# Value weights in two loads from ScalarE's queue, gate columns behind the first of them, first values in row steps

## The chip, the cores and the metric

One core of a Trainium2 chip runs the kernel. The metric is the device time of one execution in microseconds (us); the time before is 221.36, the median of three runs (221.32 to 221.83). The profile is of one execution, which took 221.32. Its times count from the first instruction; TensorE is PE, VectorE DVE, ScalarE ACT, GpSimd POOL and SyncE SP.

## What is computed

A block with two branches on one normalised input, in bf16: linear attention with a softmax feature map, and a gated bilinear unit.

```python
# x 2048 x 512, 32 heads of 16; wqkv 512 x 1536; w_gate, w_up 512 x 1792; w_down 1792 x 512
xn = layernorm(x)
q, k, v = split(xn @ wqkv)                          # 32 heads each
phi(a) = concat(softmax(a @ w_phi), softmax(-(a @ w_phi)))
kv = phi(k).T @ v ;  z = sum of phi(k) over tokens
A = (phi(q) @ kv / (phi(q) @ z + 1e-6)) @ wo
B = ((xn @ w_gate) * (xn @ w_up)) @ w_down
out = x + A + B
```

## The kernel before

**Tiles and stages.** The 2048 tokens are 16 tiles `t` of 128; the model dimension of 512 is four row blocks `q` of 128. `x_tile(t)` is loaded, normalised into `xn_tile(t)` and transposed into `xnT`, which every projection reads as its stationary or its moving operand. The values of a tile are `k_pe(t)` (L547): four matmuls of 512 columns over the four row blocks of `wv_v`, the value columns of `wqkv`, and a copy on ACT. The features of the keys need `Wp`, the key weights times `w_phi`: `wprime(1)` (L491) makes it from the transposed key weights `wT` and the block matrix `wbd` (from `w_phi`, `make_wbd`, L391). Then `k_pk(t)` and `k_norm(t)` make softmax features, `emit_kv` sums them with the values, and `q_pk` to `q_oT` do the queries. `glu(g, ft)` (L575) makes 128 of the 1792 hidden columns for 512 tokens: four matmuls with gate columns, four with up columns, a copy of the gate product on ACT, a multiply on DVE (L588). `final(t)` does both output products. There are 56 such gated units, put between the other work to fill TensorE.

**The first four tiles.** Tiles 0 to 3 (`RAW = 4`) are treated apart, to start early: `emit_centred(t)` (L416) subtracts the mean only, `emit_T(t)` (L472) transposes on TensorE with the identity `ident` and copies on ACT, and 1/sqrt(variance) is a scale of the later copies. The mean comes from DVE's statistics, `emit_moments` (L412: `bn_stats` L413 and `bn_aggr` L414), but for the tiles of `ACT_MEAN` (L410: 1 and 3) from an accumulating ACT pass (L421), and `emit_moments` follows later. Tiles 4 to 15 are normalised fully (statistics L450, L479) and transposed by DMA on SP's queue (L483).

**Zero matmuls.** 27 matmuls of zeros (L367) run on TensorE before the first data, and 8 more after the transpose of tile 1 (L724).

**The loads.** L352 to L362 issue all early loads on SP's queue. `load_x(on, t0, n, at)` loads n tiles of x, `load_w` a weight, `load_gu(on, f0, n, at)` n blocks of 128 gate columns and as many up columns (two loads), `load_wT` the key or query weights through a transposing DMA. `at` is the time in ns at which a load is said to land; it is used by the planner alone.

**The order of the work.** Nothing is ordered by hand. Every operation is a step with an engine, a cost, and dependencies from what it reads and writes; steps can be given more of them (`deps.append`). `_order` (L790) then plays the steps through: each engine is free at 850 ns at first, and takes from its steps whose dependencies are already placed the one that can start first, `max(ready, free)`, and of equal ones the one of lowest priority number (mostly the order of writing; gated units have numbers above a million and so come last). A DMA holds its queue for its `issue` cost (500 ns, 4600 ns for `load_wT`) and lands at the later of start plus 1700 ns and `at`. Steps marked `urgent`, the first four tiles' centring and transposes, are taken if they can start within 300 ns of the best one (`URGENT`, L792). The result is a fixed program for each engine, run in order with waits on semaphores (`_emit_all`): an engine whose next instruction waits does nothing else.

Of the kernel before, what the change touches and what calls it, by code (L numbers as in the profile page):

```python
# [12 lines left out]
PE, ACT, DVE, POOL, SP = "PE", "ACT", "DVE", "POOL", "SP"  # L13
# [7 lines left out]
NQ = D // 128  # L21
# [176 lines left out]
def _build(nc, es, A_x, A_wqkv, A_w_phi, A_wo, B_w_gate, B_w_up, B_w_down, out):  # L198
# [59 lines left out]
    def sbv(name, lo, n):  # L258
        off = layout[name] + lo
        return arena[:, off:off + n]  # L260
# [5 lines left out]
    def bank(b, lo=0, n=512):  # L266
        return psum[:, b * 512 + lo: b * 512 + lo + n]

    sc = _Sched(nc)


    def act_op(out_ap, in_ap, func=ACTF.Copy, scale=1.0, bias=None, prio=None):
        def fn(e):
            kw = {}
            if bias is not None:
                kw["bias"] = bias
            return e.activation(out=out_ap, in_=in_ap, func=func, scale=scale, **kw)  # L277
        r = [in_ap]
        if isinstance(scale, bass.AP):
            r.append(scale)  # L280
        if isinstance(bias, bass.AP):
            r.append(bias)
        return sc.step(ACT, fn, reads=r, writes=[out_ap], cost=(50.0 if str(in_ap.tensor.name) == "ps" else 95.0) + 0.833 * in_ap.free_size(),
                       lat=180.0, prio=prio)

    def dve(fn, reads, writes, n, rate=1.0, fixed=65.0, prio=None):
        return sc.step(DVE, fn, reads=reads, writes=writes, cost=fixed + rate * n / 0.96, lat=150.0, prio=prio)

    def pool(fn, reads, writes, n, rate=1.8, fixed=130.0, prio=None):
        return sc.step(POOL, fn, reads=reads, writes=writes, cost=fixed + rate * n, lat=120.0, prio=prio)  # L290

    def mms(items, prio=None, cold=False):

        def fn(e):
            ins = None
            for o, l, r, a, z in items:
                ins = e.matmul(o, lhsT=l, rhs=r, start=a, stop=z)  # L297
            return ins
        reads = []
        writes = []  # L300
        c = 0.0
        for o, l, r, a, z in items:
            reads += [l, r]
            writes.append(o)
            c += max(25.0, o.free_size() / 2.4 + 2.3) * (1.92 if cold else 1.0)
        return sc.step(PE, fn, reads=reads, writes=writes, cost=c, lat=260.0, prio=prio)

    def group(o, pairs):
        n = len(pairs)
        return [(o, l, r, i == 0, i == n - 1) for i, (l, r) in enumerate(pairs)]  # L310

    ident = sbv("ident", 0, 128)
    bind8 = sbv("bind8", 0, 8)
# [5 lines left out]
    def x_tile(t):  # L319
        return sbv("x", t * 512, 512)  # L320
# [3 lines left out]
    def xnT(q, s_lo, n):  # L324
        return sbv("xnT", q * S_TOK + s_lo, n)

    wT_v = sbv("wT", 0, 2 * NQ * 512).rearrange("p (w j d) -> p w j d", w=2, j=NQ)
    wv_v = sbv("wv", 0, NQ * 512).rearrange("p (q j) -> p q j", q=NQ)
# [7 lines left out]
    def load_x(on, t0, n, at):  # L336
        return sc.dma(on, sbv("x", t0 * 512, n * 512).rearrange("p (t d) -> p t d", t=n),
                      x_flat[t0 * 128:(t0 + n) * 128, :].rearrange("(t p) d -> p t d", p=128), at=at)

    def load_w(on, dst, src, at, issue=500.0):  # L340
        return sc.dma(on, dst, src, at=at, issue=issue)
# [5 lines left out]
    def load_gu(on, f0, n, at):  # L347
        return [load_w(on, v[:, :, f0 * 128:(f0 + n) * 128],
                       src[:, f0 * 128:(f0 + n) * 128].rearrange("(q p) f -> p q f", p=128), at)
                for v, src in ((wg_v, B_w_gate), (wu_v, B_w_up))]  # L350

    load_x(SP, 0, 1, 2950.0)  # L352
    load_x(SP, 1, 1, 3400.0)
    load_x(SP, 2, 2, 4700.0)
    load_w(SP, wv_v, A_wqkv[:, 1024:1536].rearrange("(q p) j -> p q j", p=128), 6500.0)
    load_gu(SP, 0, 4, 9900.0)
    load_x(SP, 4, 4, 11400.0)
    sc.dma(SP, wphi_v, bass.AP(tensor=A_w_phi.tensor, offset=A_w_phi.offset, ap=[[16, 128], [2048, NQ], [1, 16]]),
           at=11600.0)
# [5 lines left out]
    zero = sbv("tree", 0, 128)  # L365
# [4 lines left out]
    def c_fn(e):  # L370
        e.memset(ident, 0.0)
        return e.memset(bind8, 1.0)
    pool(c_fn, [], [ident, bind8], 300)

    def c2_fn(e):
        e.affine_select(out=ident, in_=ident, compare_op=ALU.not_equal, fill=1.0, base=0,
# [30 lines left out]

    RAW = 4

    ACT_MEAN = (1, 3)  # L410

    def emit_moments(t):  # L412
        dve(lambda e: e.bn_stats(stats_v[:, t, 0:6], x_tile(t)), [x_tile(t)], [stats_v[:, t, 0:6]], 512)  # L413
# [2 lines left out]
    def emit_centred(t):  # L416

        reads = [x_tile(t)]
        if t in ACT_MEAN:
            mean = lnt_v[:, 2, 8 + t:9 + t]  # L420
# [23 lines left out]
    def scale_of(t):  # L444
        return rstd_v[:, t, 0:1] if t < RAW else 1.0
# [15 lines left out]
    def xn_tile(t):  # L461
        return sbv("xn", (t % 4) * 512, 512)
# [4 lines left out]
    def next_a():  # L467
        b = a_bank[0] % a_banks[0]
        a_bank[0] += 1
        return b  # L470

    def emit_T(t):  # L472
        b = (5, 6, 7, 4)[t] if t < RAW else next_a()
        mms([(bank(b, q * 128, 128), xn_tile(t)[:, q * 128:(q + 1) * 128], ident, True, True) for q in range(NQ)],
            cold=t < 2)
        act_op(xnT_v[:, :, t * 128:(t + 1) * 128], bank(b).rearrange("p (q s) -> p q s", q=NQ))

    def emit_xn(t):
        dve(lambda e: e.tensor_scalar(out=xn_tile(t), in0=x_tile(t), scalar1=mv_v[:, t, 0:1],  # L479
                                      scalar2=rstd_v[:, t, 0:1], op0=ALU.subtract, op1=ALU.mult),  # L480
            [x_tile(t), mv_v[:, t, 0:1], rstd_v[:, t, 0:1]], [xn_tile(t)], 512, rate=0.5)
        if t >= 4:
            sc.dma(SP, xnT_v[:, :, t * 128:(t + 1) * 128], xn_tile(t), transpose=True, issue=1250.0, land=3200.0,  # L483
                   at=36000.0 + 1300.0 * (t - 8) if t >= 8 else 22900.0 + 550.0 * (t - 4))
            return
        emit_T(t)

# [58 lines left out]

    def k_pe(t):  # L547
        b = next_a()
        mms(group(bank(b), [(xnT(q, t * 128, 128), wv_v[:, q, :]) for q in range(NQ)]))
        act_op(vext_all[:, t, :, 0:64], bank(b).rearrange("p (c j) -> p c j", c=8), scale=scale_of(t))  # L550

    def k_pk(t):
# [164 lines left out]
    for t in range(RAW):  # L717
        first = len(sc.steps)
        emit_centred(t)
        emit_T(t)  # L720
        for st in sc.steps[first:]:
            st.urgent = True
        if t == 1:
            mms([(bank(7, 0, 128), zero, zero, True, True)] * 8, cold=True).deps.append(sc.by_eng[PE][-2])  # L724
        if t in ACT_MEAN:
            emit_moments(t)
        emit_root(t)
        k_pe(t)
# [60 lines left out]

def _order(sc):  # L790

    URGENT = 300.0  # L792
    n = len(sc.steps)
    remaining = [len(st.deps) for st in sc.steps]
    dependents = [[] for _ in range(n)]
    for st in sc.steps:
        for d in st.deps:
            dependents[d.idx].append(st)
    ready = {e: [] for e in sc.by_eng}
    ready_time = [0.0] * n  # L800
    for st in sc.steps:
        if remaining[st.idx] == 0:
            ready[st.eng].append((0.0, st.idx))
    free_at = {e: 850.0 for e in sc.by_eng}
    new_order = {e: [] for e in sc.by_eng}
    global_order = []
    for _ in range(n):
        best = None
        for e, lst in ready.items():
            if lst:  # L810
                fa = free_at[e]
                cand = min(lst, key=lambda p: (max(p[0], fa), sc.steps[p[1]].prio))
                soon = [p for p in lst if sc.steps[p[1]].urgent and max(p[0], fa) <= max(cand[0], fa) + URGENT]
                if soon:
                    cand = min(soon, key=lambda p: sc.steps[p[1]].prio)
                key = (max(cand[0], fa), cand[1])
                if best is None or key < best[0]:
                    best = (key, e, cand)
        if best is None:
            raise RuntimeError("scheduling deadlock")  # L820
        (start, idx), e, cand = best
        ready[e].remove(cand)
        st = sc.steps[idx]
        if isinstance(st.lane, tuple):
            free_at[e] = start + st.cost
            st.finish = max(start + st.lat, st.at)
        else:
            free_at[e] = start + st.cost
            st.finish = free_at[e] + st.lat
        st.seq = len(new_order[e])  # L830
        new_order[e].append(st)
        global_order.append(st)
        for dep in dependents[idx]:
            remaining[dep.idx] -= 1
            fin = free_at[PE] if st.lane == PE and dep.lane == PE else st.finish
            ready_time[dep.idx] = max(ready_time[dep.idx], fin)
            if remaining[dep.idx] == 0:
                ready[dep.eng].append((ready_time[dep.idx], dep.idx))
    sc.by_eng = new_order
    sc.est = {e: free_at[e] for e in free_at}  # L840
    return global_order
# [86 lines left out]
```

## Time and profile before

| | us |
|---|---|
| median of three runs | 221.36 |
| the profiled execution | 221.32 |
| its span, first to last instruction | 219.6 |
| TensorE busy | 215.9 (98% of the span), 1285 matmuls |
| VectorE busy | 192.9 (88%), 549 instructions |
| ScalarE busy | 116.7 (53%), 193 instructions |
| GpSimd busy | 10.5 (5%) |
| granted TensorE clock, mean | 1.00 |

Busy time alone says little here, since TensorE is nearly always busy: what tells is when its unbroken row of matmuls begins, when it ends, and what each matmul in it costs. A matmul of 512 columns starts 0.216 us after the one before it when the row is full. One of 128 columns starts 0.107 us after the one before it until 6.7 us, and 0.056 us after it from then on. In the early part the order of instructions on SP's queue, and the time at which each load lands, are read beside it. In the view of DMA issues the last column is the time from issue to landing; in the timeline the first two columns are start and length.

### The profile page before, as it was taken

What the parts mean: (1) busy time and instruction counts of PE and PEld (TensorE: products, weight loads), DVE (VectorE), ACT (ScalarE), POOL (GpSimd) and SP (SyncE); (2) the same over time, 40 slices, a digit from 0 to 9 for tenths busy, and PEclk for the clock granted to TensorE, in tenths of its full rate; (3) what the DMA queues carried; (4) which work ended last, traced back from release to release, by engine and by line L of the source; (5) the groups of instructions that cost most, each with busy time, mean ns of one, the idle gap of its engine ahead of it and who ended that gap; (6) DMA issues with size and microseconds to landing.
All of it is one profiled execution on the core that took longest, in us unless ns stands there. A gap on an engine that the chain in (4) does not pass through costs nothing.

```text
span 219.6 us, 3584 instructions
## 1 busy us (share of the span) xinstructions
PE 215.9 (98%) x1285; PEld 106.1 (48%) x1285; DVE 192.9 (88%) x549; ACT 116.7 (53%) x193; POOL 10.5 (5%) x29
## 2 busy tenths in 40 slices
PE   7999999999999999999999999999999999999995
PEld 7554444444445545444445544444444445444543
DVE  3578999999997489999999899999999999998432
ACT  4868986465533599965452785745453333230000
POOL 4440000200002000000000000000000000000000
DMA  6999630048400440000000003155366555856451
GB/s 165 337 292 285 132 135 0 3 96 280 150 0 4 96 96 3 0 0 0 3 0 1 3 0 59 37 96 102 84 131 99 119 119 118 102 120 142 96 75 49
DMA packets 47442, 19.91 MB, mean 91 GB/s; under 512 B 37440, under 2 KB 47424, under 8 KB 47424
## 3 DMA queue, kind: packets, MB, share of 16 engines
q1 hardware_dynamic: 47424, 19.69, 39.4%
q8 instruction: 10, 0.16, 0.3%
q14 instruction: 8, 0.07, 0.1%
HBM read 8.67 MB, written 2.10 MB: 49 GB/s over the span
## 4 chain that ended last, share of the span: by engine, by line
PE 96%; DMA 2%; DVE 1%; SPq 0%; issue 0%
PE ps L297 96%; DMA arena<-in_A_x_dram 2%; SPq L165 0%; DVE arena L413 0%; DVE arena L428 0%; DVE arena L693 0%; DVE arena L414 0%
## 5 line engine op out<-in xcount | busy, mean ns | idle before, releaser
L297 PE MATMUL ps<-arena 128*128 128x512 bf16 (+4 forms) x1285 | 215.9, 332 | 1.4 <-DVE arena L366 1.0
L297 PEld LDWEIGHTS ps<-arena 128*128 128x128 bf16 x1285 | 106.1, 99 | 111.0 <-ACT arena L277 1.1
L277 ACT ACTIVATE arena<-ps 128x512 bf16<-128x512 f32 (+1 forms) x136 | 72.1, 590 | 46.8 <-PE ps L297 38.7
L277 ACT ACTIVATE arena<-arena 128x1024 bf16<-128x1024 bf16 (+1 forms) x40 | 38.6, 978 | 28.8 <-DVE arena L523 28.7
L537 DVE TENSOR_TENSOR arena<-arena 128x512 f32<-128x512 bf16 (+3 forms) x128 | 48.9, 391 | 0.1
L588 DVE TENSOR_TENSOR arena<-ps,arena 128x512 bf16<-128x512 f32 x56 | 37.9, 677 | 4.4 <-PE ps L297 2.1
L517 DVE TENSOR_TENSOR arena<-arena 128x64 bf16<-128x64 bf16 (+3 forms) x128 | 31.3, 270 | 3.2 <-ACT arena L277 2.9
L523 DVE TENSOR_TENSOR arena<-arena 128x1024 bf16<-128x1024 bf16 x32 | 21.5, 671 | 0.1
L693 DVE TENSOR_TENSOR arena<-ps,arena 128x512 bf16<-128x512 f32 (+2 forms) x13 | 8.4, 647 | 7.1 <-PE ps L297 6.9
L564 DVE TENSOR_TENSOR arena<-arena 128x1024 bf16<-128x1024 bf16 x16 | 10.8, 677 | 0.0
L450 DVE BATCH_NORM_STATS2 arena<-arena 128x6 f32<-128x512 bf16 x12 | 8.0, 678 | 2.3 <-DMA arena<-in_A_x_dram 2.3
L277 ACT ACTIVATE arena<-ps,arena 128x512 bf16<-128x512 f32 x12 | 7.9, 682 | 2.1 <-PE ps L297 1.6
L561 DVE RECIPROCAL arena<-arena 128x64 bf16<-128x64 f32 x16 | 8.7, 541 | 0.0
L665 DVE TENSOR_TENSOR arena<-ps,arena 128x512 bf16<-128x512 f32 x12 | 8.1, 674 | 0.1
L657 DVE RECIPROCAL arena<-ps 128x32 f32<-128x32 f32 x16 | 5.5, 347 | 2.4 <-PE ps L297 2.4
L644 DVE TENSOR_TENSOR arena<-arena 128x512 bf16<-128x512 bf16 x16 | 6.6, 413 | 0.0
L641 DVE RECIPROCAL arena<-arena 128x32 f32<-128x32 f32 x16 | 5.3, 334 | 0.0
L479 DVE TENSOR_SCALAR arena<-arena 128x512 bf16<-128x512 bf16 x12 | 4.2, 405 | 1.1 <-POOL arena L458 1.1
L413 DVE BATCH_NORM_STATS2 arena<-arena 128x6 f32<-128x512 bf16 x4 | 2.7, 690 | 2.3 <-DMA arena<-in_A_x_dram 2.3
L456 POOL TENSOR_SCALAR arena<-arena 128x4 f32<-128x4 f32 x3 | 0.8, 259 | 52.4 <-DVE arena L452 52.4
L458 POOL TENSOR_TENSOR arena<-arena 128x4 f32<-128x4 f32 x3 | 3.1, 1044 | 0.3
L690 DVE SCALAR_TENSOR_TENSOR arena<-ps,arena 128x512 bf16<-128x512 f32 x4 | 3.0, 746 | 0.0
(29 smaller groups left out, 25.0 us busy)
## 6 DMA issues: line engine op xcount, KB each, us to landing
out_dram<-arena SPq DMA_DIRECT2D x15, 128.0 KB, 1.8
arena<-in_B_w_down_dram SPq DMA_DIRECT2D x1, 1792.0 KB, 7.5
arena<-in_B_w_gate_dram SPq DMA_DIRECT2D x2, 640.0 KB, 7.0
arena<-in_B_w_up_dram SPq DMA_DIRECT2D x2, 640.0 KB, 8.2
arena<-in_A_x_dram SPq DMA_DIRECT2D x1, 1024.0 KB, 5.7
arena<-arena SPq DMA_TRANSPOSE x44, 3.0
arena<-in_A_wqkv_dram SPq DMA_DIRECT2D x1, 512.0 KB, 4.4
arena<-in_B_w_gate_dram SPq DMA_DIRECT2D x1, 512.0 KB, 5.4
```

What stands on the lines that cost most here:

```text
L277: return e.activation(out=out_ap, in_=in_ap, func=func, scale=scale, **kw)
L297: ins = e.matmul(o, lhsT=l, rhs=r, start=a, stop=z)
L450: dve(lambda e, t=t: e.bn_stats(stats_v[:, t, 0:6], x_tile(t)), [x_tile(t)], [stats_v[:, t, 0:6]], 512)
L517: dve(lambda e, dst=dst, src=src, k=k: e.tensor_tensor(out=dst, in0=src[:, :, 0:k], in1=src[:, :, k:2 * k], op=ALU.max), [src], [dst], 16 ...
L523: dve(lambda e: e.tensor_tensor(out=p4, in0=p4, in1=src[:, :, None, :].to_broadcast([128, 16, 16, 4]), op=ALU.subtract), [pst, src], [pst] ...
L537: dve(lambda e, dst=dst, src=src, k=k: e.tensor_tensor(out=dst, in0=src[:, :, 0:k], in1=src[:, :, k:2 * k], op=ALU.add), [src[:, :, 0:2 * ...
L561: dve(lambda e: e.reciprocal(out=rs, in_=sm), [sm], [rs], 64, rate=6.0)
L564: dve(lambda e: e.tensor_tensor(out=e4, in0=e4, in1=r4[:, :, None, :].to_broadcast([128, 16, 16, 4]), op=ALU.mult), [ek_v[:, t, :], rs], [ ...
L588: dve(lambda e: e.tensor_tensor(out=dst, in0=bank(bu), in1=gr, op=ALU.mult), [bank(bu), gr], [dst], 512, prio=-1.0)
L644: dve(lambda e: e.tensor_tensor(out=e1, in0=e1, in1=rs[:, :, None, :].to_broadcast([128, 8, 16, 4]), op=ALU.mult), [e1, rs], [e1], 512, ra ...
L665: dve(lambda e: e.tensor_tensor(out=o4, in0=n4, in1=w4, op=ALU.mult), [nd[:, :, 0:64], w], [o], 512)
L693: dve(lambda e: e.tensor_tensor(out=og, in0=ob, in1=xs, op=ALU.add), [ob, xs], [og], c1 - c0, prio=-2.0)
```

## The change

The value weights are loaded in two halves of 256 rows (row blocks 0, 1 and 2, 3) on ACT's queue in place of one load on SP's; the first half depends on GpSimd's memset of `ident` and `bind8`. The first gate and up loads depend on the first half. For tiles 0 to 3 the four matmuls of the values become four steps in place of one, so that each can be placed, and can wait, by itself. The mean of tile 3 comes from DVE. Four zero matmuls in place of eight follow tile 1's transpose. In the planner, an urgent step on TensorE is taken ahead of another only within 50 ns, and some stated landings are new.

```diff
     load_x(SP, 0, 1, 2950.0)
     load_x(SP, 1, 1, 3400.0)
-    load_x(SP, 2, 2, 4700.0)
-    load_w(SP, wv_v, A_wqkv[:, 1024:1536].rearrange("(q p) j -> p q j", p=128), 6500.0)
-    load_gu(SP, 0, 4, 9900.0)
+    load_x(SP, 2, 2, 4900.0)
+    wv_loads = [load_w(on, wv_v[:, 2 * h:2 * h + 2, :],
+                       A_wqkv[h * 256:(h + 1) * 256, 1024:1536].rearrange("(q p) j -> p q j", p=128), at)
+                for on, h, at in ((ACT, 0, 4500.0), (ACT, 1, 6000.0))]
+    for st in load_gu(SP, 0, 4, 9300.0):
+        st.deps.append(wv_loads[0])
     load_x(SP, 4, 4, 11400.0)
...
     def c_fn(e):
         e.memset(ident, 0.0)
         return e.memset(bind8, 1.0)
-    pool(c_fn, [], [ident, bind8], 300)
+    wv_loads[0].deps.append(pool(c_fn, [], [ident, bind8], 300))
...
-    ACT_MEAN = (1, 3)
+    ACT_MEAN = (1,)
...
-                   at=36000.0 + 1300.0 * (t - 8) if t >= 8 else 22900.0 + 550.0 * (t - 4))
+                   at=36000.0 + 1300.0 * (t - 8) if t >= 8 else 23600.0 + 550.0 * (t - 4))
...
     def k_pe(t):
         b = next_a()
-        mms(group(bank(b), [(xnT(q, t * 128, 128), wv_v[:, q, :]) for q in range(NQ)]))
+        items = group(bank(b), [(xnT(q, t * 128, 128), wv_v[:, q, :]) for q in range(NQ)])
+        if t < RAW:
+            for item in items:
+                mms([item])
+        else:
+            mms(items)
...
         if t == 1:
-            mms([(bank(7, 0, 128), zero, zero, True, True)] * 8, cold=True).deps.append(sc.by_eng[PE][-2])
+            mms([(bank(7, 0, 128), zero, zero, True, True)] * 4, cold=True).deps.append(sc.by_eng[PE][-2])
...
-    URGENT = 300.0
+    URGENT = {PE: 50.0, DVE: 300.0, ACT: 300.0, POOL: 300.0, SP: 300.0}
...
-                soon = [p for p in lst if sc.steps[p[1]].urgent and max(p[0], fa) <= max(cand[0], fa) + URGENT]
+                soon = [p for p in lst if sc.steps[p[1]].urgent and max(p[0], fa) <= max(cand[0], fa) + URGENT[e]]
```

## The prediction

> **What bounds the kernel now.** I read the chain that ended last first. Its columns are start, length (us) and what held the chain:
>
> ```profile
> 6.00 0.36 DVE arena L428
> 6.41 210.94 PE ps L297 x1242
> 217.37 0.29 DVE arena L693
> ```
>
> From 6.41 to 217.34 TensorE runs without a break; only the fronts of 6.41 and the tail of 2.3 us are something else. So TensorE's work after 6.41 can't shrink, and the time moves by two things alone: when useful matmuls begin, and any hole that is put into the row. Everything that the diff touches lies before 20 us, so I read next what SP's queue issues there (start, length of the issue, what):
>
> ```profile
> 2.17 0.47 SPq L165 DMA_DIRECT2D arena<-in_A_wqkv_dram  x1
> 2.68 0.51 SPq L165 DMA_DIRECT2D arena<-in_B_w_gate_dram  x1
> 3.23 0.51 SPq L165 DMA_DIRECT2D arena<-in_B_w_up_dram  x1
> 3.78 0.51 SPq L165 DMA_DIRECT2D arena<-in_A_x_dram  x1
> 4.33 0.92 SPq L165 DMA_DIRECT2D arena<-in_A_w_phi_dram  x1
> 5.30 5.69 SPq L164 DMA_TRANSPOSE arena<-in_A_wqkv_dram  x1
> 11.04 0.57 SPq L165 DMA_DIRECT2D arena<-in_B_w_gate_dram  x1
> 11.66 0.50 SPq L165 DMA_DIRECT2D arena<-in_B_w_up_dram  x1
> ```
>
> and when these loads land (last column: us from issue to landing; 512 KB are the first columns, 640 KB the later ones):
>
> ```profile
> arena<-in_B_w_gate_dram SPq DMA_DIRECT2D x1, 512.0 KB, 5.4
> arena<-in_B_w_up_dram SPq DMA_DIRECT2D x1, 512.0 KB, 6.4
> arena<-in_A_x_dram SPq DMA_DIRECT2D x1, 512.0 KB, 7.4
> arena<-in_A_wqkv_dram SPq DMA_TRANSPOSE x1, 7.8
> ...
> arena<-in_B_w_gate_dram SPq DMA_DIRECT2D x1, 640.0 KB, 5.3
> arena<-in_B_w_up_dram SPq DMA_DIRECT2D x1, 640.0 KB, 6.5
> ```
>
> Issue plus landing: first gate columns 8.1, first up columns 9.6, x tiles 4 to 7 11.1, the transposed key weights 13.1, the next gate columns 16.3, the next up columns 18.1. When does TensorE want them? By the engines that take its results, the copy of the first gate product and the multiply of the first up product:
>
> ```profile
> 11.54 0.60 ACT L277 ACTIVATE arena<-ps 128x512 bf16<-128x512 f32 x1 [0.17 <-PE ps L297]
> 12.40 0.69 DVE L588 TENSOR_TENSOR arena<-ps,arena 128x512 bf16<-128x512 f32 x1
> ```
>
> They stand 0.86 apart, four matmuls of 512 columns at 0.216. The trace's single matmuls begin at 10.48 (gate) and 11.34 (up). So the gate columns have 2.4 us to spare today and the up columns 1.7.
>
> **The order on SP: the step that decides.** The diff makes both first loads of the gated unit depend on the first half of the value weights. The planner gives each engine the ready step that can start first, and only ties go by priority. I worked its rule through by hand, for the order alone. SP is free at 850 + 3 x 500 = 2350 after the three early x loads. Gate and up are ready at 4500 (the half's stated landing); x tiles 4 to 7, the phi weights and the transposed load are ready at 0. So these three go first, at 2350, 2850 and 3350; the last is charged 4600, SP is free at 7950, and only then come gate and up. The new order is x 0-3, x 4-7, phi, the transposed load, gate, up. On ACT the second half (no dependency) is ready at 850 and goes ahead of the first half, which waits for GpSimd's memset of ident, planned to finish at 1640 (it ends near 1.03 us in the trace). Both halves are issued by about 2 us.
>
> **The sum.**
> - x and the value weights. Gate landed at 8.1 after 512 KB of x, 512 of value weights and 512 of gate. Afterwards 1024 KB of x and 512 of value weights are the same 1.5 MB. Upper end 8.1. Lower end: the slow start (529 KB from 2.0 to 4.5, where each half microsecond from 5.0 to 6.5 moves about 187) vanishes with two queues, 406 KB less to wait for, 1.1 us: 7.0. I take 7.9, near the upper end, since the 1 MB load that starts on idle queues near 25.5 us climbs as slowly (37, 115, 195, 338, 385 GB/s in half microseconds) though much is queued.
>
> The Trainium skill, DMA: Bandwidth & Descriptors, section Issuing engines are not separate DMA queues, speaks against a gain here: loads issued from ScalarE and SyncE run on the same 16 DMA engines and interleave, and a second issuer only saves issue time. By that rule the first term is 8.1 and the time 0.2 more; no run here shows two issuers yet.
>
> - The transposed load lands 13.1 - 11.1 = 2.0 after x 4-7: 9.9 (9.0 to 10.1). Its issue took 5.69 with 2.5 MB ahead of it and 1.90 on an idle queue (at 77 us), so SP comes free between about 5.6 and 8.0.
> - Gate follows it. The row that is alike is the next gate load: issued the moment the transposed load's issue was over, landed 16.3 - 13.1 = 3.24 later, against 1.81 for the equal up load behind it. The stretch after the transposed load shows why (PE's columns first, last column GB/s):
>
> ```profile
> 12.50:13.00 0.50, 0.50 (x4) 0.21 (x3) 0.50 (x1) 0.00 (x0) 0.42 (x2) 1.00 1.02 77
> 13.00:13.50 0.50, 0.50 (x5) 0.20 (x2) 0.50 (x2) 0.23 (x1) 0.32 (x1) 1.00 0.56 115
> 14.00:14.50 0.50, 0.50 (x12) 0.50 (x11) 0.50 (x2) 0.14 (x1) 0.00 (x0) 1.00 1.03 381
> ```
>
>   512 KB in place of 640 take 1.81 / 5 = 0.36 less: 2.88. If gate is queued early enough that there is no slow start, 1.45. I take 2.88, as SP again comes free some 1.5 us before the transposed data ends. Gate 12.8.
> - Up: 1.45 (four fifths of 1.81) behind it, 14.2. Ends: 9.0 + 1.45 + 1.45 = 11.9 and 10.1 + 2.88 + 1.52 = 14.5 (1.52 is 9.62 - 8.10).
>
> The first up matmul starts at 14.2 in place of 11.34: **+2.9 us** (0.6 to 3.2). All that is behind it on TensorE's in-order queue, the transformed key weights and every later product, moves by as much, and as the row has no slack nothing is won back. The profiled execution took 221.32 with a span of 219.6 (1.7 around it) and is within 0.04 of the median of 221.36: 221.32 + 2.9 = **224.2**.
>
> **What costs nothing, and its cover.**
> - Values in row steps, half the weights early, tile 3's mean on VectorE: x tiles 2 and 3 share the queues with the value weights and may land up to 1.4 later than 5.03 (at 6.4, where 1 MB has moved). Tile 3 was at TensorE 1.77 after its landing; its statistics and aggregate, now behind tile 2's on VectorE, add 0.69 + 0.18 and about 0.2 of hand-over. Its transpose then is near 9.2 and the last values near 10.9. The wait for gate until 12.8 hides this; without that cover it costs 0 to 0.5, against 10.48 today. A start of the values before 7.02 would end in the same wait, so its gain, 0.65 at most, is swallowed.
> - Four zero matmuls fewer: 4 x 0.107 = 0.43, between 5.06 and 6.41 where TensorE waits for tile 2 anyway.
> - ACT's two issues: about 2 x 0.47 = 0.94. Its table load (1.28, now 0.78 to 2.06) ends near 3.0 if it moves behind them, and x tile 1 isn't there before 3.39.
> - Behind the waiting gate on SP stand the four later gate and up loads. SP is free near 8.0 and not 11.04, so these aren't later than today. VectorE's first multiply now waits until 15.2; behind it are the statistics of tiles 4 to 7 and so their transposes (SP, 18.05), up to 2.9 later, as are their users on TensorE.
> - By the planner's times two gated units end at 13.1, ahead of the 13.6 it gives the transposed weights, so a third gate product may come before these. That permutes TensorE's work and starts the softmax chain 0.86 later; 0 to +0.86, taken as 0 since TensorE has gated units to fill with.
>
> **Rivals.**
> - *The data is there earlier* (no slow start behind the transposed load, or two queues start faster). For: the later up load shows 1.81 without a pause. Against: both starts from idle seen above. With 7.9 + 2.0 + 1.45 + 1.45 up lands at 12.8: +1.45, 222.8; at the lowest 11.9: 221.9.
> - *TensorE's clock falls back in the stall.* Of 128-column matmuls the first start 0.107 apart, after 6.7 us 0.056. The values would end near 10.9 and gate come at 12.8, up at 14.2: two idle pieces, 1.9 and 0.5. The slow spacing lasted 5.7 us at the start; if it returns for as long, half of that is lost, so the price is 0 to 2.8; TensorE wouldn't be starting from rest, so I take the middle: +2.9 + 1.4, 225.6. For: the row never had such a hole. Against: the granted clock reads 1.00 throughout, and the work before would have been dense. The Trainium skill, TensorE: Matmul & The Clock Gate, Part 1, has the clock halved by an idle window of about 3.4 us, longer than either piece; by that rule this rival would not come about, and no run here shows it.
> - *Faster: the change does what its words say.* If gate and up land before TensorE has finished the values, the stall is not there, and the values pull forward: of the 1.35 us from 5.06 to 6.41 (zero matmuls and idle) three value matmuls at the slow 0.427 fill 1.28, and 3 x 0.216 = 0.65 leave the row: 220.7. It decides from an up landing of 10.7 on. For: gate would be queued from about 5 us if SP kept the written order. Against: the planner's rule, and 1 MB of x and key weights ahead of it.
>
> **How the numbers follow.** Forecast 0.57, earlier data 0.22, slow clock 0.14, faster 0.07. The likeliest case alone spans 223.4 to 224.6. 0.3% is 0.66 us, about what a measurement of this kernel can tell from no change. Faster 0.06 (all but the edge of the last case); same 0.08 (a third of the earlier-data case, below 222.0, and that edge); slower 0.86. The range 222.0 to 226.0 leaves out the faster case, the lowest part of the second and the upper part of the third.
>
> **What would show it.** SP's rows: x 4-7, phi and the transposed load ahead of gate. Landings: transposed near 10, gate near 12.8, up near 14.2. TensorE idle, released by the two weight loads, some 2 us between 10 and 14.2, then one row to the end, with 0.216 spacing. It is wrong if gate is issued before x 4-7, or if the first up product is multiplied before 13, or if a second hole opens after 20 us.

## The result and the profile after

The changed kernel takes 224.48 us (median of six executions, 223.84 to 226.5), the kernel before 221.38 beside it (six, 220.99 to 221.83): a ratio of 1.0158, 95% interval 1.0137 to 1.0179, 3.1 us slower. Two of the six executions, 226.15 and 226.5, have a mean granted TensorE clock of 0.992, the other four 1.000; where the clock goes is asked in the experiments. The profiled execution took 223.84 with a span of 222.1, 2.5 more than the profile before.

The chain that ended last, after (start, length, what held it):

```profile
3.24 4.41 SPq L164
...
8.31 5.04 DMA arena<-in_B_w_up_dram
13.35 0.05 issue
13.40 206.02 PE ps L297 x1214
219.41 0.02 issue
219.44 0.29 DVE arena L701
```

Before, TensorE's row was the chain from 6.41 on. Now the issue of the transposed load and the up columns hold it until 13.40, the first up matmul. Then 206.0 us of TensorE work follow; before, it was 206.0 too, from the first up matmul at 11.34 to 217.34. So the row itself is what it was and ends 2.06 later (219.4), and behind it lie 2.70 us in place of 2.26 (the tail, in which the last output is stored). These two, 2.06 and 0.44, are the whole difference of the two profiles.

SP's timeline after (start, length of the issue, what):

```profile
0.78 1.86 SPq L165 DMA_DIRECT2D arena<-in_A_x_dram  x4
2.69 0.51 SPq L165 DMA_DIRECT2D arena<-in_A_w_phi_dram  x1
3.24 4.41 SPq L164 DMA_TRANSPOSE arena<-in_A_wqkv_dram  x1
7.69 0.57 SPq L165 DMA_DIRECT2D arena<-in_B_w_gate_dram  x1
8.31 0.50 SPq L165 DMA_DIRECT2D arena<-in_B_w_up_dram  x1
```

This is the order the prediction worked out: all of x, phi, the transposed load, and only then gate and up, whose issue began at 2.68 and 3.23 before. The view of DMA issues after (last column: us from issue to landing):

```profile
arena<-in_A_wqkv_dram ACTq DMA_DIRECT2D x2, 256.0 KB, 3.6
arena<-in_A_x_dram SPq DMA_DIRECT2D x1, 512.0 KB, 5.5
arena<-in_B_w_gate_dram SPq DMA_DIRECT2D x1, 512.0 KB, 4.1
arena<-in_B_w_up_dram SPq DMA_DIRECT2D x1, 512.0 KB, 5.0
...
arena<-in_A_wqkv_dram SPq DMA_TRANSPOSE x1, 6.5
```

Issue plus landing: x 4 to 7 at 7.65, the transposed weights at 9.74, gate at 11.83, up at 13.35. The second half of the value weights is issued first, as predicted, and the halves are there at 4.04 and 5.16, where one load landed at 6.60. The users of the gated unit, the copy of the gate product and the multiply of the up product:

```profile
13.38 0.61 ACT L277 ACTIVATE arena<-ps 128x512 bf16<-128x512 f32 x1
...
14.47 0.69 DVE L596 TENSOR_TENSOR arena<-ps,arena 128x512 bf16<-128x512 f32 x1 [3.98 <-PE ps L297]
```

The first multiply starts at 14.47 in place of 12.40. And behind the transposed load the slow start is there, but shorter (window, then busy time of PE, PEld, DVE, ACT and POOL, granted clock, DMA share, GB/s):

```profile
9.00:9.50 0.50, 0.50 (x2) 0.15 (x1) 0.39 (x3) 0.50 (x2) 0.13 (x2) 1.00 0.89 74
9.50:10.00 0.50, 0.50 (x3) 0.22 (x2) 0.27 (x2) 0.14 (x1) 0.42 (x2) 1.00 0.63 135
10.00:10.50 0.50, 0.50 (x5) 0.22 (x4) 0.49 (x1) 0.00 (x0) 0.50 (x2) 1.00 0.93 305
10.50:11.00 0.50, 0.50 (x7) 0.29 (x5) 0.00 (x0) 0.21 (x1) 0.42 (x2) 1.00 1.09 387
```

The PE column shows a second thing: 2 or 3 matmuls in half a microsecond. In this execution the value matmuls of 512 columns start 0.427 apart until 10.36, and only then 0.216. (The clock column reads 1.00 all the same; before the spacing halves it tells nothing, here as in the other profiles, so for the start the spacing is read as the clock, and the moment at which it halves is called the moment of the full clock.) So the values end at 12.32 and TensorE hardly waits for gate. That leaves two causes that would both look like this: the landings, or the values at half speed.

### The profile page after: what moved, and what is told of

It reads as the page before. It is cut to its first block, busy times and chain, and to the rows that moved or that the text cites. A ratio compares the mean times of both kernels' runs of the same rounds, so it can differ in the third digit from the quotient of the medians.

```text
span 222.1 us, 3572 instructions
## 1 busy us (share of the span) xinstructions
PE 217.3 (98%) x1281; PEld 106.2 (48%) x1281; DVE 193.1 (87%) x549; ACT 115.6 (52%) x191; POOL 10.7 (5%) x29
## 4 chain that ended last, share of the span: by engine, by line
PE 93%; SPq 3%; DMA 2%; issue 0%; DVE 0%
PE ps L297 93%; DMA arena<-in_B_w_up_dram 2%; SPq L164 2%; SPq L165 1%; DVE arena L701 0%
## 5 line engine op out<-in xcount | busy, mean ns | idle before, releaser
L572 DVE TENSOR_TENSOR arena<-arena 128x1024 bf16<-128x1024 bf16 x16 | 10.9, 679 | 0.0
```

What stands on the lines that cost most here:

```text
L572: dve(lambda e: e.tensor_tensor(out=e4, in0=e4, in1=r4[:, :, None, :].to_broadcast([128, 16, 16, 4]), op=ALU.mult), [ek_v[:, t, :], rs], [ ...
```

## The experiments

Four theories. The hold is the dependency of the first gate and up loads on the first half of the value weights. **Landing:** the hold lets the planner put gate and up behind the transposed load, and the landing of up sets the row. **Slow values:** the row starts late since the values run at half speed. **Sharing:** value weights on ACT's queue delay the x tiles. **Idle clock:** the idle time that the hold makes costs clock as well. Times are medians; ratios are against the kernel before on the same chip.

### The hold taken out: a_unheld

```diff
-    for st in load_gu(SP, 0, 4, 9300.0):
-        st.deps.append(wv_loads[0])
+    load_gu(SP, 0, 4, 9300.0)
```

> The changed kernel without the hold: the first gate and up loads depend on nothing, so SP issues them right behind x tiles 2 and 3, ahead of x tiles 4 to 7, the phi weights and the transposed key weights. All else as changed. In the changed kernel's profile TensorE wants the first up columns at 13.18 us (the values end at 12.32, after 16 matmuls of which half run at 0.427 us) and gets them at 13.35. Theory 1, the landings set the time: up lands near 10, the first up product starts at 11.4 or earlier and the time falls to 221.8 or less. Theory 2, TensorE's slow spacing up to 10.3 us sets it and the landing adds only 0.2: the first up product starts near 13.2 and the time stays at 223.6 or so.

222.54 (221.91 to 223.57, twelve executions), ratio 1.0048 (1.0031 to 1.0065): between what the two theories gave. Its DMA issues:

```profile
arena<-in_B_w_gate_dram SPq DMA_DIRECT2D x1, 512.0 KB, 6.0
arena<-in_B_w_up_dram SPq DMA_DIRECT2D x1, 512.0 KB, 7.0
```

Issued at 2.18 and 2.69, they land at 8.19 and 9.68, as before the change (8.1 and 9.6), and in the profiled execution TensorE's row ends at 217.37, as before; the end of its chain:

```profile
213.98 3.40 PE ps L297 x31
217.41 0.29 DVE arena L700
```

So by the medians the hold and the order it causes are 1.1% of the 1.6%. The other 0.5% is in the rest of the diff.

### The hold kept, the written order forced: a_turn

The planner may place x 4 to 7 and every later load on SP only after the held gate and up loads.

```diff
-    load_x(SP, 4, 4, 11400.0)
+    load_x(SP, 4, 4, 11400.0).behind = held[1]
...
```

> The changed kernel with the hold kept, but the planner lets x tiles 4 to 7 and every load written behind them on SP take their turn only after the first gate and up loads: SP waits for the first half of the value weights (5.2 us) with nothing else to issue. Gate issued near 5.2 lands near 8.3, up near 9.8, x tiles 4 to 7 near 11.3, the transposed key weights near 13.3. Theory 1: the stall is gone, 221.8 or less. Theory 2: 223.6, as without the hold. If waiting on SP costs by itself, the transposed weights land after 14 and the time is above that of the run without the hold.

223.0 (221.67 to 223.83), ratio 1.0064 (1.0041 to 1.0088), above the 221.8 of the landing theory. SP's timeline:

```profile
5.10 0.37 SPq L166 DMA_DIRECT2D arena<-in_B_w_gate_dram  x1
5.52 0.51 SPq L166 DMA_DIRECT2D arena<-in_B_w_up_dram  x1
6.07 0.51 SPq L166 DMA_DIRECT2D arena<-in_A_x_dram  x1
```

Gate now really waits for the first half (5.10), lands at 8.96 and up at 10.47, and TensorE, busy from 5.60 on, waits for neither. The row still ends 1.05 later than a_unheld's (218.42): in this execution the slow spacing lasts until 8.9, in a_unheld's until 4.9, and there is no wait for gate left that would cover it. In the medians the wait alone is 0.16% from no hold at all (1.0064 and 1.0048, intervals that overlap); nearly all of the hold's 1.1% is the order.

### The values made fast: a_zeros and a_unheld_zeros

More zero matmuls, to have the full clock sooner; in the second kernel without the hold.

```diff
-    mms([(bank(7, 0, 128), zero, zero, True, True)] * 27, cold=True)
+    mms([(bank(7, 0, 128), zero, zero, True, True)] * 34, cold=True)
...
+        if t == 0:
+            fill = mms([(bank(7, 0, 128), zero, zero, True, True)] * 5, cold=True)
...
```

> The changed kernel with more zero matmuls: 34 in place of 27 at the start, and 5 between the transposes of tiles 0 and 1, so that TensorE rests less between 3.9 and 5.7 us. Loads as changed. Theory 2 with nothing else: the short spacing is back at 6.7 us, the values end near 10.9 and the time falls by 1.5 or more, to 222.3 or less. Theory 1: the values end early but gate and up still land at 11.8 and 13.35, TensorE stands idle before them and the time stays at 223.8 (223.4 to 224.5). If each of the two alone is enough to hold the row, this one and the run without the hold both change little.

224.42 (224.2 to 224.65), ratio 1.0132 (1.0109 to 1.0155). The full clock is there from 3.75 and the values end near 11.3, a microsecond sooner. TensorE's timeline:

```profile
8.46 2.99 PE L297 MATMUL ps<-arena 128*128 128x128 bf16 x16 [0.81 <-DVE arena L431]
12.02 1.04 PE L297 MATMUL ps<-arena 128*128 128x512 bf16 x4 [0.56 <-DMA arena<-in_B_w_gate_dram]
13.52 3.66 PE L297 MATMUL ps<-arena 128*128 128x512 bf16 x28 [0.47 <-DMA arena<-in_B_w_up_dram]
```

The microsecond won is lost again in two waits, 0.56 for gate and 0.47 for up, and the row starts at 13.52 in place of 13.40. Slow values falls as the cause; landing stands.

> Both edits: no hold, and the added zero matmuls. If the time is the later of the two (landing of up, end of the slow values), this one gains what neither of the others does: values end near 10.9, no wait for gate or up, the first up product near 11.8 or before, 221.2 to 222.2. If theory 1 alone holds it is no better than the run without the hold; if theory 2 alone holds, no better than the run with the zeros.

222.71 (222.55 to 223.07), ratio 1.0055 (1.0037 to 1.0073): a miss. With fast values and no hold it is still no better than a_unheld. The planner put tile 3's transpose, not ready before 8.46, ahead of values that were; TensorE stands 0.81 there, and its row ends at 218.14.

### The hold alone, on the kernel before: b_hold and b_hold_fill

```diff
-    load_w(SP, wv_v, A_wqkv[:, 1024:1536].rearrange("(q p) j -> p q j", p=128), 6500.0)
-    load_gu(SP, 0, 4, 9900.0)
+    wv_load = load_w(SP, wv_v, A_wqkv[:, 1024:1536].rearrange("(q p) j -> p q j", p=128), 6500.0)
+    for st in load_gu(SP, 0, 4, 9900.0):
+        st.deps.append(wv_load)
```

> The kernel before with the hold alone: the first gate and up loads depend on the one load of the value weights (all on SP), so the planner puts x tiles 4 to 7, the phi weights and the transposed weights ahead of them. Nothing else of the change. Theory 1 (the reordering on SP is the loss): value weights land at 6.6, transposed weights near 10, gate near 12.2, up near 13.7; the values end near 10.5, TensorE idles some 1.7 us ahead of gate and 0.6 ahead of up, and the time is 223.3 to 224.5. If the loss needs the value weights on ScalarE's queue or the late x tiles too, it stays under 222.3.

225.83 (224.46 to 226.0), ratio 1.0194 (1.0171 to 1.0217): more than expected. The profiled execution, at clock 1.000, took 224.46, inside what was expected; the other four took 225.54 to 226.0 at clock 0.992. TensorE's timeline of the profiled one:

```profile
6.36 4.15 PE L297 MATMUL ps<-arena 128*128 128x128 bf16 x24 [0.81 <-DVE arena L429]
12.98 1.04 PE L297 MATMUL ps<-arena 128*128 128x512 bf16 x4 [2.46 <-DMA arena<-in_B_w_gate_dram]
14.47 2.77 PE L297 MATMUL ps<-arena 128*128 128x512 bf16 x12 [0.46 <-DMA arena<-in_B_w_up_dram]
```

Gate lands at 12.93 and up at 14.42; the row from 14.47 is 206.01 long once more. The values end at 10.51 and TensorE stands still for 2.46. To see whether this stillness takes the clock in the other executions, 46 zero matmuls fill it, put by a dependency between the last values and the first gate product; nothing else is changed:

```diff
+    last_value = sc.by_eng[PE][-1]
+    fill = mms([(bank(7, 0, 128), zero, zero, True, True)] * 46)
+    fill.deps.append(last_value)
...
```

> The kernel before with the hold alone, as in the run before, and 46 zero matmuls of 128 columns between the last values and the first gate product (2.6 us at 0.056), so that TensorE isn't at rest in the stall. They add to no result and end about when gate lands. With the hold alone the profiled execution had two idle pieces (2.6 and 0.6 us) and took 224.46, with a mean granted clock of 1.00; the other four took 225.5 to 226.0 with a mean clock of 0.992, which is what one window of 3.4 us at half speed makes of 222. Theory, idleness takes the clock away: here all runs are near 224.5 with clock 1.00, a median 1.0 or more under that of the hold alone. Rival, the clock falls for another reason (the run, the chip): still 225.5 to 226 in most.

224.38 (224.29 to 224.6), ratio 1.0133 (1.012 to 1.0146), all four at clock 1.000. Of the waits for loads one is left (us in total, times, longest):

```profile
PE ps L297 <- DMA arena<-in_B_w_up_dram: 0.4, 1, 0.4
```

Up lands at 14.09, little sooner than under b_hold, and the median is 1.45 lower. So idle clock is shown: idle time in this place costs not only itself but, in four of five executions, some clock. Chance or the chip is an unlikely rival: the two kernels ran on two chips, and of the executions of the kernel before beside them, 23 and 15, none lost the clock.

### Sharing: a_unheld_sp, b_act_wv, a_unheld_mean3

The rest of the diff with both halves on SP's queue, in row order, without the hold:

```diff
-                for on, h, at in ((ACT, 0, 4500.0), (ACT, 1, 6000.0))]
+                for on, h, at in ((SP, 0, 5800.0), (SP, 1, 6500.0))]
...
```

> The changed kernel without the hold and with both halves of the value weights on SP behind x tiles 2 and 3, in row order, not on ScalarE's queue; row steps, means and zero matmuls as changed. It asks where the 0.5% that is left without the hold comes from. Theory 3, sharing: the halves travel with x and hold x tiles 0 to 3 back by 0.5, 1.0 and 0.8 us; then here x tiles 2 and 3 land at 5.0 as before, the transposes follow earlier by 0.8 and the time is 220.7 to 221.6. Theory 4, the work: tile 3's mean on VectorE and the row steps cost it; then the time stays at 222.3 to 222.7.

221.39 (220.72 to 222.22, twelve executions), ratio 1.0005 (0.9992 to 1.0018): the time before. So the 0.5% goes with the ACT queue. Its chain:

```profile
2.68 4.91 DMA arena<-in_A_wqkv_dram
...
7.64 209.91 PE ps L297 x1235
```

Tiles 2 and 3 land at 4.68 here, at 5.85 in the changed kernel. But this doesn't show that the late tiles are the cost. In the profiled executions the row ends at 217.54 here and at 217.37 in a_unheld, whose tiles are late; what a_unheld's loses against this one (222.09 against 221.56) is lost in a tail of 3.0 us in place of 2.3. The other way round, the kernel before with its one value load on ACT's queue and nothing else:

```diff
-    load_w(SP, wv_v, A_wqkv[:, 1024:1536].rearrange("(q p) j -> p q j", p=128), 6500.0)
+    load_w(ACT, wv_v, A_wqkv[:, 1024:1536].rearrange("(q p) j -> p q j", p=128), 6500.0)
```

> The kernel before with its one load of the value weights on ScalarE's queue and nothing else changed. Two readings. Sharing: x tile 0 lands near 3.3, tile 1 near 4.4, tiles 2 and 3 near 5.9 in place of 2.8, 3.4 and 5.0, the transposes of tiles 2 and 3 and all behind them come 0.7 to 0.9 later, 222.0 to 222.5; if the earlier landing of the value weights (near 5.2 for 6.6) counts for more than x, the time is 221.4 or less. Tail: SP has one instruction less; if the last output is held up because a fetch of SP's instructions falls on it, it lands 1.8 to 2.1 us after issue as in the kernels with two loads on ScalarE's queue, or 1.44 if one instruction is not enough to move that fetch.

224.67 (224.15 to 225.42), ratio 1.0147 (1.0129 to 1.0165), far above what was expected. x tile 1 lands at 5.44 in place of 3.39, tiles 2 and 3 at 6.19 in place of 5.03. TensorE's timeline and, below it, its windows (columns as above):

```profile
6.71 0.84 PE L297 MATMUL ps<-arena 128*128 128x128 bf16 x12 [1.93 <-DVE arena L428]
```

```profile
4.10:7.51 3.41, 1.20 (x16) 0.90 (x16) 1.37 (x5) 2.02 (x6) 0.89 (x2) 1.00 1.10 361
7.51:10.93 3.42, 3.06 (x15) 1.64 (x15) 2.59 (x10) 1.72 (x4) 2.15 (x6) 0.50 1.16 307
10.93:14.34 3.41, 3.41 (x17) 1.55 (x16) 1.16 (x2) 2.52 (x4) 1.85 (x5) 1.00 1.04 253
```

The late tile leaves TensorE idle for 1.93 in one piece and busy for 1.20 of 3.41; the granted clock of the next 3.42 is 0.50, and then 1.00 again. That half-clock stretch is 1.7 us of lost work, 0.8% of the span: the 0.992. Two of the four executions show it; the other two (225.42 and 224.15) are no shorter, and where theirs went no profile shows.

Whether tile 3's mean on DVE, in place of ACT, is part of the 0.5%:

```diff
-    ACT_MEAN = (1,)
+    ACT_MEAN = (1, 3)
```

> The changed kernel without the hold and with tile 3's mean on ScalarE again, as before the change; halves on ScalarE's queue. Theory 4 (the mean on VectorE): tile 3's transpose is up to 1.0 us earlier than 8.5, and the time falls from 222.5 to 221.5 to 222.0. Theory 3 (sharing): 222.3 to 222.7, as without this edit, because ScalarE's pass over tile 3 stands in the way of the copies of the first transposes instead.

223.25 (222.28 to 223.81), ratio 1.0084 (1.0061 to 1.0106): no better than a_unheld, so no cost of the mean on DVE is to be seen. What the edit itself does stays open. In its profiled execution tiles 2 and 3 landed at 6.85 (5.87 in a_unheld), the slow spacing lasted until 9.5, and the row ended at 218.95:

```profile
5.92 213.03 PE ps L297 x1250
```

The profiles of a_unheld, a_turn and this kernel have the full clock at 4.9, 8.9 and 9.5 and end their rows at 217.37, 218.42 and 218.95. Without the wait for gate as a cover, the moment of the full clock moves the row, and differences of half a per cent between these kernels can't be put down to their edits alone.

### Halves and row steps alone, and both kernels again

The kernel before with two halves on SP, row steps for tiles 0 to 3 and the window of 50 ns:

```diff
+    for h, at in ((0, 5600.0), (1, 6600.0)):
+        load_w(SP, wv_v[:, 2 * h:2 * h + 2, :],
...
+            for item in items:
+                mms([item])
```

> The kernel before with only the parts that looked free: value weights in two loads of 256 rows on SP, the first values in row steps and the 50 ns window for urgent steps on TensorE; eight zero matmuls, tile 3's mean on ScalarE, no hold, nothing on ScalarE's queue. If the row steps have a gain of their own, two value matmuls of tile 0 run ahead of the third transpose and the unbroken row ends 0.2 to 0.5 earlier: 220.8 to 221.2. If the second load's landing eats it, 221.3 to 221.7.

222.21 (221.8 to 222.85), ratio 1.0033 (1.0021 to 1.0044). TensorE's waits for loads:

```profile
PE ps L297 <- DMA arena<-in_A_wqkv_dram: 1.4, 1, 1.4
```

The second half lands at 8.41, where one load lands at 6.60: the row steps begin early and then wait for it. They have no gain of their own here. Why the second half is late (7.59 in a_unheld_sp too) stays open.

Both kernels once more, unchanged, to see how far the early stretch differs between executions:

> The kernel before, once more, for two readings that one profile can't give. First the tail: in its profile the last output landed 1.44 us after its issue, in the changed kernel and in the four runs so far 1.8 to 2.1. If that belongs to the changed kernel, 1.44 comes back here; if it is scatter, something from 1.4 to 2.1 shows. Second the moment at which TensorE's spacing halves: 6.7 us in the first profile, 10.4, 4.9, 3.8, 4.2 and 8.9 in the others. Theory 2a, it is set by how densely TensorE works: 6.7 again. Theory 2b, it falls differently in each execution: another moment from 4 to 9 us, and little change of the time, since the values wait for their weights until 7.0. Time 221.2 to 221.6.

221.28 (median of twelve, 220.89 to 224.61), ratio 0.9993 (0.9978 to 1.0008). One of the twelve, 224.61, has a clock of 0.992: without the hold this kernel can lose a window too. The short spacing begins at 5.03 here, at 6.7 in the first profile, and the row ends at 217.4 in both.

> The changed kernel once more, for a second profile and more executions. In its first profile the spacing was 0.427 us until 10.4, so the values ended at 12.3 and TensorE idled only 0.3 us before the up columns; two of six executions took 226.2 and 226.5 with a mean granted clock of 0.992. If the moment of the clock varies by execution and the landing of up sets the row, the first up product starts within 0.2 of the landing of up (13.2 to 13.6) whatever the spacing was before, executions with clock 1.00 lie at 223.8 to 224.6, and a part of them, with 0.992, lies 1.5 to 2.3 above. If the slow values set the time, executions with an early clock are under 223.3.

224.42 (223.89 to 224.9), ratio 1.0133 (1.0111 to 1.0155), all four at clock 1.000. The profiled execution took 224.69; TensorE's timeline:

```profile
12.71 1.04 PE L297 MATMUL ps<-arena 128*128 128x512 bf16 x4 [0.99 <-DMA arena<-in_B_w_gate_dram]
14.20 2.98 PE L297 MATMUL ps<-arena 128*128 128x512 bf16 x13 [0.45 <-DMA arena<-in_B_w_up_dram]
```

Here the full clock came at 8.88, the values ended near 11.5, and TensorE waits for both loads; the first up matmul starts 0.05 behind the landing of up, as the landing theory has it. x 4 to 7 landed at 8.35, transposed weights 10.42, gate 12.66, up 14.15: 0.8 later than in the first profile of the same kernel, 0.7 of it before x 4 to 7 was in.

No kernel of these beats the one before; the best, a_unheld_sp, equals it.

## Why the prediction was right, and which terms were off

**The mechanism and the time are right:** 224.2 was forecast, 224.48 measured, and the first up matmul, forecast for 14.2, came at 13.40 and 14.20 in the two profiles. The order on SP is the one worked out by hand, ACT's second half goes first, and b_hold, a_unheld and a_turn show that this order, more than the wait, costs the time. a_zeros shows that the landing of up sets the row.

**The first term.** x and values landed: 7.9 taken, 7.65 and 8.35 measured. The Trainium skill, DMA: Bandwidth & Descriptors, section Issuing engines are not separate DMA queues, says two issuers share the same 16 engines. The landings agree: the same 1.5 MB took until 8.10 before, and with the value weights on a second queue the x tiles pay (tile 1 at 4.42 in place of 3.39).

**The transposed load:** 2.0 taken; 9.74 - 7.65 = 2.09 and 10.42 - 8.35 = 2.07. Its issue ended at 7.65 and 8.31 (between 5.6 and 8.0 was forecast). The 2.5 MB that the prediction puts ahead of it in the kernel before are what had been issued; 0.5 MB of them, x tiles 0 to 3, had landed by 5.03.

**Gate behind it is the mis-sized term:** 2.88 taken, 2.09 and 2.24 measured (2.24 in b_hold, too). A slow start is there, against the 1.45 of the rival without one, but costs some 0.65 to 0.8 and not 1.43. It was priced from a later load 640 KB large; the windows there climb from 77 and 115 GB/s, here from 74 and 135 to 305 and 387.

**Up:** 1.45 taken, 13.35 - 11.83 = 1.52 and 1.49.

**What was to cost nothing.** "The wait for gate hides" the values held, and had to hide more than was thought: in the first profile the values ran at half speed until 10.36 and ended at 12.32, 0.5 behind gate's landing, and yet up at 13.35 covered them. Its four fewer zero matmuls were priced by their length alone; whether they made the clock late isn't settled, since it came at 10.36 and 8.88 in the same kernel. ACT's table load moved behind its two issues and ended at 3.08, before x tile 1 was in. x tiles 2 and 3 at 6.4 was an upper end: they landed at 5.85 in both profiles, and tile 3 was centred by 8.4. Yet its transpose, forecast near 9.2, came at 10.36 and 9.60, since in the program it stands behind values that ran at half speed; the last values, forecast near 10.9, ended at 12.32 and near 11.5. The prediction had no term for a full clock that comes later than 6.7. The third gate product did come ahead of the transformed weights, as the prediction allowed for: 16 matmuls of 512 columns lie between 13.40 and the first of 128 columns at 16.86, where 12 lay between 11.34 and 13.93 before. The row behind the first up matmul is 206.0 all the same, so taking this as 0 was right.

**What the sum left out:** the tail, +0.44, which the prediction names (2.3 us) and takes as unchanged; it makes up for half of the gate term in the first profile (2.06 + 0.44 = 2.5 against 2.9). That the time came out so near is in this part luck. Against the median the forecast is 0.3 low.

**The rivals.** *Data earlier* gave 222.8; the time that gate takes behind the transposed load (2.09 and 2.24) lies about midway between its 1.45 and the forecast's 2.88. *Clock falls back* was given 225.6 and a chance of 0.14 by two idle pieces of 1.9 and 0.5. It is real, but belongs to single executions: of the ten executions of the changed kernel that were timed, two show 0.992 and took 226.15 and 226.5. Under b_hold it is four of five, and filling the idle time ends it. The Trainium skill, TensorE: Matmul & The Clock Gate, Part 1, has the clock halved by an idle window of some 3.4 us; the traces agree on the length (3.41) but not on idle: a window with TensorE busy for 1.20 lost it. *Faster* needed up to land by 10.7; a_turn's lands at 10.47 and is still 0.6% slower than before. a_unheld's lands at 9.68 and is 0.5% slower. So the point from which it was to decide was passed in two kernels and no gain came: early values, the rival's other half, won nothing in any run (in a_unheld they start at 6.1 in place of 7.0, and the row ends where it did).

## What to carry to other kernels

A dependency given to one load in a planned order is not only a wait: the planner fills the wait with whatever is ready, and a long transposing issue that jumps the queue costs more than the wait did. When a load is moved to a second engine's queue, ask which load now shares the DMA engines with it; here it is the x tiles that everything starts from. And price idle time near the start of a kernel twice, once as time and once as clock.

## What the hardware showed that was not expected

**The clock goes with how busy TensorE was in a window.** The half-clock stretch of b_act_wv is one window of 3.41 us. At the start, windows of 3.41 with TensorE busy 2.43, 2.50 and 2.65 were not followed by the full clock, ones with 2.71, 3.00, 3.19 and more were. The two nearest to each other are of after_again (full clock at 8.88) and a_zeros (at 3.75):

```profile
2.06:5.47 3.41, 2.65 (x24) 2.11 (x21) 1.49 (x4) 1.96 (x4) 1.06 (x3) 1.00 1.00 327
```

```profile
0.34:3.75 3.41, 2.71 (x26) 2.71 (x27) 0.62 (x2) 1.28 (x1) 1.49 (x11) 1.00 0.51 156
```

Once given, the clock outlived windows with 2.32 and 1.57 busy (b_hold, cut at 8.19, 11.61 and 15.0), and was lost after one with 1.20; behind the end of a_turn's row it was lost after one with 1.27 (217.14 to 220.55). So the moment of the full clock, 3.75 to 10.4 over these profiles, and the loss under b_hold can hang on where the cuts fall in an execution; the cuts are read back from the matmul spacing, and the profile of an execution of b_hold that lost the clock wasn't taken.

**The longer tail goes with an instruction fetch.** In all eight profiles of kernels with a load on ACT's queue the last output lands 1.8 to 2.1 after its issue, in all six without one 1.4 to 1.5. The DMA view of the stretch behind the last matmul, after (packets, MB, share; last line us to landing) and a_unheld_sp:

```profile
q1 hardware_dynamic: 288, 0.13, 16.5%
q14 instruction: 1, 0.01, 0.9%
...
out_dram<-arena SPq DMA_DIRECT2D x1, 32.0 KB, 1.8
```

```profile
q1 hardware_dynamic: 288, 0.13, 19.5%
...
out_dram<-arena SPq DMA_DIRECT2D x1, 32.0 KB, 1.5
```

One packet of the instruction queue, 8 KB, falls into this stretch in all eight and in none of the six. In the changed kernel it holds one DMA engine for 0.4 us ahead of its share of the last output. The last packets of that output end only some 0.1 us later than before (1.55 behind the row, not 1.45), so what takes the rest of the 0.4 isn't seen, and that the packet is the cause isn't shown. In these kernels SP's program is one load shorter and ACT's one or two longer, either of which could shift the fetches; neither was tried by itself. The tails are 0.4 to 0.8 us longer in the eight; that is most of what a_unheld's profiled execution (tail 3.0 against 2.26) lost.

**Two halves on one queue** land their second half at 7.59 and 8.41, one load of the same bytes at 6.42 to 6.76; the cause is open.
